# A gated-attention and MLP kernel: second unit's keys loaded alone, and the first 230 entries of a written order made anew

## Chip, cores and metric

The kernel runs on one core of a Trainium2 chip. The metric is the device time of one execution in microseconds (us). Engines are named as in the profile: PE (TensorE; PEld is its weight load), DVE (VectorE), ACT (ScalarE), POOL (GpSimd) and SP (SyncE, which here only issues DMAs).

## What is computed

A gated linear attention over 4 batches, 8 heads, 768 steps of 48 values feeds a gated two-layer MLP (3072 tokens, 384 to 2048 to 384). Cut to its core:

```python
f = 1 / (1 + exp(-f_logit))
for t in range(768):
    state = f[t] * state + outer(k[t], v[t])     # per batch and head, 48 x 48
    y[t] = q[t] @ state
x = y over all heads                              # 3072 tokens x 384
h = x @ w_in                                      # 384 -> 2048
g = h * clip(h + 3, 0, 6) / 6
out = g @ w_out                                   # 2048 -> 384
```

## The kernel before

**Units.** The attention is cut into 24 units, one batch and one chunk of 128 steps each. Units 0 to 3 are the first chunk of the four batches. For unit i, `load.i`, `loadq.i` and `loadv.i` are DMAs of gate logits, of queries with keys (one DMA of 512 KB into a tile `qkf`, rotated over four buffers) and of values. `loadq` of unit 0 is split: `loadk.0` brings its keys, `loadq.0` its queries.

On the engines a unit is this chain: ACT `gate` (sigmoid), DVE `back` (a scan of the gates backward, into `suffix`), `rend` (reciprocal of the end), `kmul` (keys times suffix, line 446), `fwd` (a forward scan, line 457), `qmul` (queries times it, line 463); PE `tk` (transposes keys, line 527), ACT `ktok` (copies them out), PE `kv` (keys by values, line 548), ACT `carry0`, `carry1`; PE `att` (keys by queries, line 508), DVE `mask` (line 515), PE `qs` (state part, line 583), `av` (line 599); then `xh`, `xs`, `xl` write the result as two float16 parts, and `hole` moves rows by DMA.

**Weights.** `ld.f` loads weight tile f (16 of them); ACT `cy`, `z`, DVE `mid`, `dif`, `top`, ACT `high` and DVE `lowi` turn it into two float16 parts. `high` gives the upper part, `lowi` the lower.

**MLP.** `mm1a.f` (line 844) multiplies units 0 and 1 by weight tile f, `mm1b.f` units 2 and 3; each is nine matmuls, of which only the last three read the lower weight part. `relua`, `ga` and `mm2a` (line 862) follow on ACT, DVE and PE. Later entries of the MLP have other names.

**Fillers.** `warm.n` (line 1087) is a matmul of zeros of n times 128 columns, n over 4 in pieces of 512; its result is not read. Each piece is two PE instructions in the profile, so `warm.16` is eight.

**Order.** One list of names, `ORDER`, fixes the order in which instructions are written. Every engine executes its own in that order, so an instruction that waits holds back all behind it on that engine; the engines meet by semaphores alone. A number after a second dot is the PSUM bank. `ON_POOL` names the entries that go to POOL instead of DVE; `kmul.1` is one of them.

Of the kernel before, what the change touches and what calls it, by code (L numbers as in the profile page):

```python
# [58 lines left out]
load.3 warm.3 kv.1.3 z.0 mid.0 loadq.2 gate.3 end.2 back.3 ld.1 carry0.1 warm.1 qs.1.0 dif.0 kmul.2 top.0 fwd.2 xl.0
carry1.1 loadq.3 av.1 hole.0 tk.2.4 rend.3 xh.1 xs.1 xl.1 z.1 qmul.2 warm.5 att.2.2 kmul.3 cy.1 mid.1 fwd.3 ktok.2  # L60
loadv.2 high.0 warm.4 kv.2.1 carry0.2 end.3 tk.3.4 ktok.3 mask.2 load.4 gate.4 qs.2.0 hole.1 av.2 xh.2 carry1.2 lowi.0
mm1a.0.4 relua.0 dif.1 qmul.3 top.1 high.1 ga.0 loadv.3 xs.2 att.3.2 mask.3 kv.3.1 ld.2 carry0.3 carry1.3 lowi.1 xl.2
loadq.4 warm.1 qs.3.2 av.3 xh.3 mm1a.1.4 cy.2 xs.3 xl.3 relua.1 z.2 back.4 kmul.4 rend.4 fwd.4 ga.1 decay.4 mm2a.0
qmul.4 load.5 gate.5 tk.4.1 mm2a.1 ktok.4 loadv.4 ld.3 cy.3 z.3 hole.2 mid.2 dif.2 top.2 att.4.2 kv.4.3 hole.3 mm1b.0.0
high.2 back.5 mid.3 relub.0 loadq.5 mm1b.1.1 relub.1 lowi.2 gb.0 dif.3 kmul.5 rend.5 gb.1 mm1a.2.4 mm1b.2.0 top.3
mm2b.0 mm2b.1 fwd.5 tk.5.1 relua.2 relub.2 gb.2 qmul.5 ld.4 z.4 cy.4 mid.4 mm2b.2 high.3 ktok.5 lowi.3 ga.2 mm1b.3.0
load.6 gate.6 loadq.6 dif.4 back.6 top.4 load.7 mm1a.3.4 ld.5 relub.3 mm2a.2 relua.3 ga.3 high.4 gb.3 cy.5 z.5 mask.4
mm2a.3 lowi.4 mm1a.4.1 relua.4 rend.6 ld.6 mm1b.4.4 relub.4 loadv.6 gate.7 loadq.7 mm2b.3 carry0.4 kmul.6 fwd.6 mid.5
ga.4 dif.5 z.6 qmul.6 top.5 cy.6 tk.6.1 ktok.6 mm2a.4 back.7 ld.7 decay.5 high.5 qs.4.2 decay.6 att.5.0 gb.4 av.4
kv.6.1 carry1.4 lowi.5 mm1.5.4 mask.5 mm2b.4 carry0.6 xh.4 z.7 xl.4 mid.6 dif.6 kmul.7 carry1.6 loadv.5 kv.5.3 ld.8  # L70
relu.5 g.5 mm2x.5 cy.7 top.6 high.6 cy.8 rend.7 tk.7.0 mid.7 dif.7 load.8 lowi.6 carry0.5 top.7 mm1.6.4 ktok.7 qs.5.2
fwd.7 qmul.7 high.7 loadv.7 relu.6 g.6 z.8 decay.7 att.6.0 ld.9 lowi.7 gate.8 av.5 cy.9 z.9 mask.6 mm1.7.4 relu.7 mid.8
dif.8 top.8 mid.9 carry1.5 dif.9 high.8 low.8 mm2x.6 mm1.8.0 g.7 loadq.8 ld.10 top.9 xh.5 cy.10 relu.8 high.9 back.8
rend.8 mm2x.7 ld.11 xl.5 g.8 att.7.2 z.10 cy.11 qs.6.0 kv.7.3 mid.10 load.10 loadv.8 av.6 dif.10 low.9 top.10 z.11
mid.11 gh.8 mm1.9.4 ld.12 ld.14 xh.6 xl.6 gl.8 mm2.8 dif.11 high.10 low.10 relu.9 g.9 cy.12 mm1.10.1 top.11 mask.7
kmul.8 carry0.7 gh.9 gl.9 hole.4 relu.10 high.11 mm2.9 carry1.7 g.10 low.11 z.12 mid.12 ld.13 dif.12 top.12 cy.13 gh.10
gl.10 tk.8.1 ktok.8 mm1.11.0 z.13 high.12 qs.7.2 mm2.10 av.7 loadq.9 ld.15 kv.8.3 decay.8 relu.11 mid.13 dif.13 low.12
loadv.9 mm1.12.1 g.11 gh.11 xh.7 top.13 carry0.8 high.13 xl.7 hole.7 gl.11 relu.12 z.14 z.15 low.13 fwd.8 qmul.8 mm2.11
g.12 gh.12 mm1.13.4 relu.13 g.13 cy.14 gh.13 gl.13 gl.12 mm2.12 cy.15 qs.8.2 mid.14 dif.14 att.8.0 mask.8 lowo.0 top.14
high.14 hole.6 hole.5 mm1.16.4 load.9 mid.15 mm1.17.1 relu.16 carry1.8 relu.17 dif.15 ws1.0 g.16 mm1.20.0 g.17 loadq.11  # L80
low.14 gate.10 xtop.0 gate.9 mm1.18.1 load.11 top.15 relu.18 loadq.10 back.9 high.15 gh.16 av.8 back.10 mm1.14.4 g.18
mm2.13 lowo.4 gh.17 relu.14 low.15 g.14 gh.14 mm1.15.1 mm1.19.4 lowo.6 gh.18 kmul.9 gl.18 rend.9 relu.15 g.15 lowo.3
gh.15 gl.14 gl.15 tk.9.1 lowo.5 lowo.1 mm2.14 fwd.9 mm2.15 gl.16 ktok.9 gl.17 outs.2 loadv.11 lowo.7 outv.1 outs.0
mm1.23.1 mm2.16 gate.11 lowo.2 ws2.0 relu.19 od.0 ws3.0 mm2.17 rend.10 xh.8 g.19 back.11 od.2 kmul.10 relu.20 decay.9
relu.23 kmul.11 hole.8 fwd.10 rend.11 od.1 load.13 qmul.10 xsum.0.2 g.20 g.23 mm1.21.4 relu.21 load.12 xleast.0 tk.10.3
ws4.0 qmul.9 decay.10 ktok.10 mm2.18 gh.19 g.21 mm1.25.3 gh.20 mm1.24.2 gh.21 loadv.10 gate.12 wtop.4 gl.19 relu.24
att.9.1 relu.25 kv.9.0 gl.20 fwd.11 g.25 carry0.9 loadv.12 g.24 wsh.0 load.14 qmul.11 mm1.22.4 gate.13 relu.22 back.12
gh.24 mm2.19 tk.11.3 gl.21 ws1.1 mask.9 gh.23 carry1.9 ktok.11 mm2.20 g.22 qs.9.0 att.11.3 gate.14 loadq.12 gh.25 gl.25
av.9 att.10.2 mm2.21 back.13 gh.22 xh.9 gl.23 kv.11.0 rend.12 kv.10.1 gl.22 mask.10 loadq.13 decay.11 mm1.26.4 ws2.1
mask.11 carry0.10 qs.10.3 ws3.1 carry0.11 carry1.10 kmul.12 kmul.13 fwd.12 qs.11.1 av.10 av.11 relu.26 mm2.22 ws4.1  # L90
xh.10 xh.11 decay.12 rend.13 mm1.27.3 gl.24 carry1.11 relu.27 loadq.14 decay.13 fwd.13 tk.12.2 mm1.28.1 relu.28 hole.9
ktok.12 wsl.0 ws1.2 g.27 tk.13.0 mm2.23 qmul.12 qmul.13 wsh.1 hole.10 att.13.3 ws2.2 g.26 ktok.13 g.28 xtop.1 att.12.1
t0.4 loadv.13 kv.12.2 kv.13.0 back.14 carry0.13 load.15 hole.11 load.16 xsum.1.4 carry0.12 gh.26 mm2.24 gh.27 mm2.25
t0.5 mask.13 carry1.12 t1.4 t1.5 seed.0.2 kmul.14 mm1.30.3 gh.28 t2.4 ws3.2 xleast.1 carry1.13 t2.5 th.4 ws4.2 gate.15
mask.12 gl.26 gl.27 wsl.1 th.5 ws1.3 mm2.26 tl.4 mm1.29.1 tk.14.2 relu.30 mm1.31.0 tl.5 relu.29 rend.14 g.30 p1.8.4
loadv.14 ktok.14 ws2.3 relu.31 p7.8.2 g.29 wsh.2 cs.8 ca.8.2 loadv.17 mm2.27 g.31 p6.8 gh.29 gate.16 fwd.14 qs.13.0
xtop.2 cx.8.3 qs.12.1 p2.8 wsl.2 ws3.3 ra.8 back.15 gl.28 p5.8 av.13 av.12 mm2.28 gh.31 gaw.8 loadq.15 loadq.17 gh.30
ws4.3 rend.15 load.17 ce.8 wsh.3 p4.8 qmul.14 gl.30 gl.29 xh.13 xh.12 p3.8 p8.8 rb.8 rx.8 p7.9.1 decay.14 wsl.3 mm2.29
gl.31 kmul.15 loadq.16 re.8 tk.15.0 gew.8 cs.9 p1.9.4 gbw.8 ca.9.2 mm2.30 fwd.15 loadv.15 gxw.8 back.16 ktok.15
xsum.2.1 mm2.31 p6.9 qmul.15 p7.11.0 xmost.2 gh.33 gh.34 cs.11 xleast.2 p2.9 decay.15 gl.34 hole.13 gh.32 kv.15.1  # L100
kv.14.0 kmul.16 cx.9.3 gl.32 outs.5 load.18 ra.9 hole.12 carry0.14 carry1.14 p4.9 carry0.15 outs.3 carry1.15 p5.9 rx.9
att.14.0 gaw.9 att.15.1 ce.9 outv.4 gate.17 p8.9 mask.14 rend.16 p3.9 mask.15 gh.35 gate.18 qs.15.0 back.17 re.9
qs.14.1 gxw.9 fwd.16 kmul.17 gl.33 gl.35 mm2.32 av.14 av.15 gew.9 p7.10.3 xh.15 rend.17 loadq.18 mm2.33 mm2.34 t0.6
p1.10.4 rb.9 mm2.35 gbw.9 qmul.16 fwd.17 xh.14 loadv.16 back.18 gh.37 gh.38 rend.18 cs.10 decay.16 load.19 kmul.18
ca.10.2 gl.38 hole.15 p6.10 gh.36 tk.17.0 gl.37 p2.10 hole.14 decay.17 tk.16.1 gh.39 cx.10.3 gl.36 p4.10 t1.6 gate.19
fwd.18 ra.10 gaw.10 t2.6 ktok.17 p5.10 ktok.16 att.16.0 kv.16.1 mm2.36 ce.10 t0.7 qmul.17 p8.10 load.20 rx.10 re.10
load.21 qmul.18 back.19 loadv.18 p3.10 mm2.37 rb.10 mask.16 gew.10 carry0.16 carry1.16 p1.11.4 gbw.10 gh.40 att.17.0
gxw.10 kv.17.1 t1.7 th.6 loadq.19 ca.11.2 gl.40 gl.39 mm2.38 gh.42 p6.11 t2.7 carry0.17 xtop.3 carry1.17 gl.42 gate.21
# [1146 lines left out]
```

## Time and profile before

| what | value |
|---|---|
| median of 3 runs | 457.13 us (456.36 to 457.28) |
| the profiled execution, device time | 456.43 us |
| its span, first to last instruction | 454.7 us |
| PE busy | 446.9 us, 98% of the span |
| DVE, ACT, POOL busy | 357.5, 232.1, 18.7 us |
| granted TensorE clock, mean | 1.000 |

The span leaves out 1.7 us of the device time around the first and last instruction. A busy PE is not PE at its peak, and fillers count as busy too. Starts and durations in the rows are in us from the span's start. A DVE or ACT row's duration runs some 0.1 us past the start of an independent follower, since such instructions overlap at their ends.

### The profile page before, as it was taken

Reading aid. Unit: us, or ns where it says so; the run is one execution under the profiler, and the core shown is the slowest. Engines: PE = TensorE matmul, PEld = TensorE weight load, DVE = VectorE, ACT = ScalarE, POOL = GpSimd, SP = SyncE. Lnnn points to the kernel's source line nnn. Section 1 sums busy time; section 2 is a strip of 40 time slices with the busy share of each in tenths; the row PEclk is TensorE's granted clock in tenths of the full one; section 3 lists DMA queues with packets and bytes.
Section 4 is the critical chain, followed back from the end, with each engine's and each line's share of the span. In section 5 each row is a group of like instructions: output and inputs, shape, how many; then the busy total and the mean of one; then the engine's idle time right before and its main releaser. Section 6 shows DMA issues by size and latency. Waiting matters only on the chain.

```text
span 454.7 us, 12561 instructions
## 1 busy us (share of the span) xinstructions
PE 446.9 (98%) x5449; PEld 290.4 (64%) x5449; DVE 357.5 (79%) x639; ACT 232.1 (51%) x393; POOL 18.7 (4%) x31
## 2 busy tenths in 40 slices
...
GB/s 281 252 237 404 201 208 240 200 172 0 62 135 80 180 31 100 69 9 115 91 0 85 99 139 1 25 140 1 2 10 1 7 28 1 1 115 2 1 0 74
DMA packets 25675, 43.18 MB, mean 95 GB/s; under 512 B 2576, under 2 KB 17424, under 8 KB 25616
## 3 DMA queue, kind: packets, MB, share of 16 engines
...
q8 instruction: 43, 0.70, 0.6%
...
q14 instruction: 16, 0.13, 0.1%
...
## 4 chain that ended last, share of the span: by engine, by line
PE 95%; DMA 1%; DVE 1%; SPq 1%; ACT 1%; issue 0%; POOL 0%; POOLq 0%
PE o L725 36%; PE pair L788 16%; PE single L788 9%; PE pair L676 7%; PE single L676 5%; PE o L862 3%; PE pair L508 3%; PE pair L599 3%; PE pair L583 3%; PE pair L548 2%; PE o L736 2%; PE pair L527 2%; DMA qkf<-qk 1%; PE o_half L878 1%; PE pair L878 1%; PE single L844 1%
## 5 line engine op out<-in xcount | busy, mean ns | idle before, releaser
L725 PE MATMUL o<-gg,weight 128*128 128x512 f16 x744 | 173.4, 379 | 0.0
L725 PEld LDWEIGHTS <-weight 128*128 128x128 f16 x744 | 71.7, 98 | 73.8
L788 PEld LDWEIGHTS <-weight 128*128 128x128 f16 x672 | 65.0, 98 | 13.2
L788 PE MATMUL pair<-xmem,wide 128*128 128x256 f16 x384 | 51.2, 273 | 0.0
L699 ACT ACTIVATE gg<-raws 128x512 f16<-128x512 f32 x64 | 38.6, 626 | 22.8 <-PE o_half L878 7.2
L788 PE MATMUL single<-xmem,weight 128*128 128x256 f16 x384 | 49.8, 273 | 0.0
L817 ACT ACTIVATE raws<-pair,half 128x512 f32<-128x512 f32 x32 | 21.6, 687 | 42.5 <-PE pair L788 33.6
L788 PEld LDWEIGHTS <-wide 128*128 128x128 f16 x384 | 36.9, 98 | 8.7 <-DVE single L803 0.6
L817 ACT ACTIVATE raws<-single,half 128x512 f32<-128x512 f32 x32 | 22.0, 689 | 38.4 <-PE single L788 37.4
L676 PEld LDWEIGHTS <-weight 128*128 128x128 f16 x243 | 23.1, 98 | 26.7 <-issue 0.3
L788 PE MATMUL pair<-xmem,weight 128*128 128x256 f16 x288 | 36.5, 273 | 0.0
L709 DVE TENSOR_TENSOR gg<-raws,gg 128x512 f16<-128x512 f32 x48 | 31.9, 684 | 5.2 <-ACT gg L699 5.1
L822 DVE SCALAR_TENSOR_TENSOR raws<-raws,single 128x512 f32<-128x512 f32 x32 | 21.8, 683 | 17.5 <-ACT raws L817 17.5
L676 PE MATMUL pair<-xmem,weight 128*128 128x512 f16 x144 | 33.2, 379 | 0.0
L803 DVE TENSOR_TENSOR pair<-pair,raws 128x512 f32<-128x512 f32 x16 | 11.1, 696 | 26.7 <-PE pair L788 23.6
L457 DVE TENSOR_TENSOR_SCAN suffix<-gates,rend 112x516 f32<-112x516 f32 x24 | 29.7, 1237 | 0.8 <-POOL qkf L446 0.7
L822 DVE SCALAR_TENSOR_TENSOR raws<-raws,pair 128x512 f32<-128x512 f32 x32 | 21.5, 681 | 10.6 <-ACT raws L817 10.4
L433 DVE TENSOR_TENSOR_SCAN suffix<-gates,unit 112x516 f32<-112x516 f32 x23 | 28.1, 1224 | 0.0
L676 PE MATMUL single<-xmem,weight 128*128 128x512 f16 x99 | 23.2, 380 | 0.0
L686 ACT ACTIVATE tg<-pair,half 128x512 f32<-128x512 f32 x16 | 10.9, 688 | 19.4 <-PE pair L676 16.2
L699 ACT ACTIVATE gg<-tg 128x512 f16<-128x512 f32 x24 | 14.4, 627 | 8.9 <-DVE tg L690 5.2
L515 DVE TENSOR_TENSOR a<-pair,causal 128x512 f32<-128x512 f32 x24 | 16.3, 683 | 1.9 <-PE pair L548 1.0
...
## 6 DMA issues: line engine op xcount, KB each, us to landing
...
gates<-fg SPq DMA_DIRECT2D x23, 258.5 KB, 3.4
...
```

Of the source, the lines that this page charges most:

```text
L433: nc.vector.tensor_tensor_scan(flat(sf)[:, ::-1], gt[:, 1:][:, ::-1], flat(unit)[:, ::-1], 0.0, op0=ALU.mult, op1=ALU.add,)
L457: nc.vector.tensor_tensor_scan(flat(sf), gt[:, :NP * (C + 1)], flat(rend), 0.0, op0=ALU.mult, op1=ALU.add,)
L508: nc.tensor.matmul(d["at"][HC * odd:HC * (odd + 1), e, 2 * n + c], t[rs, 1, n, c, odd], t[rs, 0, n, c, odd], start=not growing[at], stop=T ...
L515: nc.vector.tensor_tensor(d["a"].rearrange("r p e t -> r e p t"), d["at"], causal.unsqueeze(1).unsqueeze(1).broadcast_to([128, 2, NP, HC]) ...
L583: nc.tensor.matmul(d["y"][to:to + m, odd, n, cs], before[rs, p, :m], t[rs, 0, n, c, odd], start=alone and (odd, e) not in seen, stop=False ...
L676: nc.tensor.matmul(h, win[:, f, a, k * 128:(k + 1) * 128], g["xt"][:, k, :g["n"] // C, b], start=i == 0, stop=i == 3 * KT - 1,)
L699: nc.scalar.activation(as_t(d, 0), d["t"], AF.Copy)
L709: engine("gl", int(g["name"]) * NF + f).tensor_tensor(as_t(d, 1), d["t"], as_t(d, 0), op=ALU.subtract)
L725: nc.tensor.matmul(g["o"][m], wout[:, f, a, m * 128:(m + 1) * 128], g[f]["gg"][:, b], start=f == 0 and i == 0, stop=f == NF - 1 and i == 2 ...
L788: nc.tensor.matmul(to[:, n * 256:(n + 1) * 256], weights(q, n, a), g["wide"][:, :, block - 3, b], start=fresh and count == 1, stop=count = ...
L817: nc.scalar.activation(to, src, AF.Relu, bias=half, scale=RISE)
L822: nc.vector.scalar_tensor_tensor(to, to, TOP, src, op0=ALU.min, op1=ALU.mult)
```

## The change

The order list has one more entry, `loadk.1`, and its first 230 entries (229 before) stand in another order. From `cy.6 tk.6.1 ktok.6` on, its last 1335 entries are the same, one by one. The fillers are the same ten, but six more of them stand ahead of `tk.0`. `loadk` is offered for unit 1 too, so that unit 1's keys and queries come in two DMAs of 256 KB, the keys ahead of unit 2's gates. `kmul.1` leaves `ON_POOL` and is done on DVE.

```diff
 ON_POOL = """
-kmul.1 decay.4 kmul.6 lowi.5 kmul.7 decay.7 lowi.7 kmul.8 gl.9 decay.8 gl.11 qmul.8 gl.12 lowo.0 low.14
+decay.4 kmul.6 lowi.5 kmul.7 decay.7 lowi.7 kmul.8 gl.9 decay.8 gl.11 qmul.8 gl.12 lowo.0 low.14
 """.split()
 ORDER = """
-load.0 loadh.0 gate.0 gateh.0 back.0 backh.0 loadk.0 load.1 loadv.0 loadq.0 rend.0 end.0 kmul.0 fwd.0 gate.1 back.1
-warm.16 tk.0.3 ktok.0 warm.4 kv.0.1 carry0.0 load.2 qmul.0 warm.1 att.0.0 loadq.1 ld.0 rend.1 qs.0.2 mask.0 gate.2
...
+load.0 loadh.0 gate.0 gateh.0 back.0 backh.0 loadk.0 load.1 loadv.0 loadq.0 rend.0 gate.1 warm.16 warm.4 warm.1 warm.1
+kmul.0 warm.3 end.0 warm.3 warm.1 tk.0.3 loadk.1 load.2 loadq.1 ktok.0 fwd.0 loadq.2 loadv.1 load.3 back.1 warm.5
...
@@ -413,7 +413,7 @@
         def loadq():
-            if i:
+            if i > 1:
                 loadk(slice(0, 2))
             else:
                 nc.sync.dma_start(out=whole[i][:, 0], in_=qk[u][:, 0])
@@ -474,7 +474,9 @@
         if i == 0:
-            ops.update(halved(sf, gt, rows), loadk=loadk)
+            ops.update(halved(sf, gt, rows))
+        if i < 2:
+            ops["loadk"] = loadk
```

The DMAs on SP near the program's start, as a difference. `qkf_137` is unit 0's tile of queries and keys, `qkf_204` (before) and `qkf_161` (now) unit 1's, `qkf_168` unit 2's, `gates_80` unit 2's gates.

```order
 L423 DMA v_140<-v 128x400
 L419 DMA qkf_137<-qk 128x512
+L412 DMA qkf_161<-qk 128x512
 L408 DMA gates_80<-fg 128x517
-L412 DMA qkf_204<-qk 128x1024
+L419 DMA qkf_161<-qk 128x512
+L412 DMA qkf_168<-qk 128x1024
+L423 DMA v_170<-v 128x400
```

Unit 1's keys now go out one place earlier and alone, its queries follow unit 2's gates, and unit 2's tile comes ahead of the first weight tile, which moves behind the units' loads.

PE at its start, before: fillers (`idle`), the transposes `tk.0`, a filler, and the first two of `kv.0`.

```order
L1087 MATMUL idle<-blank 128x512 x4
L527 MATMUL pair_71<-ident,qkf_137 128x112 x4
L1087 MATMUL idle<-blank 128x512
L548 MATMUL pair_70<-v_140,ktok_157 64x48
L548 MATMUL pair_70<-v_140,ktok_157 48x48
```

PE at its start, now, to the same place:

```order
L1089 MATMUL idle<-blank 128x512 x5
L1089 MATMUL idle<-blank 128x128 x2
L1089 MATMUL idle<-blank 128x384 x2
L1089 MATMUL idle<-blank 128x128
L529 MATMUL pair_71<-ident,qkf_137 128x112 x4
L1089 MATMUL idle<-blank 128x512
L1089 MATMUL idle<-blank 128x128
L550 MATMUL pair_70<-v_140,ktok_165 64x48
```

Six fillers (one of 512 columns, three of 128, two of 384) moved ahead of `tk.0`, and the one between `tk.0` and `kv.0` is longer by 128 columns. Behind `kv.0` no filler is left until `av.2`, where before there were seven.

DVE from unit 1's `back` to unit 1's reciprocal and mask, before (`a_216` and `a_271` are what `mask.0` and `mask.1` write):

```order
L433 SCALAR_TENSOR_TENSOR suffix_79<-gates_78,unit 112x516
L463 TENSOR_TENSOR qkf_137<-qkf_137,suffix_77 112x512
L451 RECIPROCAL rend<-suffix_79 112x4
L515 TENSOR_TENSOR a_216<-pair_70,causal 128x2x4x64
L457 SCALAR_TENSOR_TENSOR suffix_79<-gates_78,rend 112x516
L463 TENSOR_TENSOR qkf_204<-qkf_204,suffix_79 112x512
L433 SCALAR_TENSOR_TENSOR suffix_81<-gates_80,unit 112x516
L515 TENSOR_TENSOR a_271<-pair_70,causal 128x2x4x64
```

The same stretch of DVE now, where the two masks write `a_237` and `a_279`:

```order
L433 SCALAR_TENSOR_TENSOR suffix_79<-gates_78,unit 112x516
L463 TENSOR_TENSOR qkf_137<-qkf_137,suffix_77 112x512
L451 RECIPROCAL rend<-suffix_79 112x4
L446 TENSOR_TENSOR qkf_161<-qkf_161,suffix_79 112x512
L457 SCALAR_TENSOR_TENSOR suffix_79<-gates_78,rend 112x516
L517 TENSOR_TENSOR a_237<-pair_70,causal 128x2x4x64
L463 TENSOR_TENSOR qkf_161<-qkf_161,suffix_79 112x512
L433 SCALAR_TENSOR_TENSOR suffix_81<-gates_80,unit 112x516
L517 TENSOR_TENSOR a_279<-pair_70,causal 128x2x4x64
```

`kmul.1` (line 446) is new on DVE, and `fwd.1` stands ahead of `mask.0`. Further on, all DVE work of units 2 and 3 down to `mask.2` stands ahead of `mid.0`, the first weight entry on DVE. The next DVE entries are `mid.0 qmul.3 dif.0 top.0 mid.1 dif.1 top.1 lowi.0 mask.3 back.4 ga.0 lowi.1`, where before `mid.0` followed `rend.2`, and `back.4` stood behind `lowi.1`.

## Rows read from the trace of the kernel before

**Rows 1.** Windows: busy time of each engine, granted clock, DMA share, GB/s.

```profile
28.86:50.37 21.51, 21.51 (x211) 18.54 (x205) 20.89 (x42) 16.59 (x28) 2.30 (x2) 1.00 0.72 277
```

**Rows 2.** Chain that ended last, 3 to 14 us: start, us, what.

```profile
3.62 0.43 SPq L408
...
4.09 5.57 DMA qkf<-qk
...
9.80 1.19 POOL qkf L446
```

**Rows 3.** DMA issues between 3.6 and 4 us: size, us to landing.

```profile
gates<-fg SPq DMA_DIRECT2D x1, 258.5 KB, 4.8
```

**Rows 4.** Timeline of PE: start, us, instructions, idle before and its releaser.

```profile
1.13 5.09 PE L1087 MATMUL idle<-blank 128*128 128x512 f32 x8 [1.13 <-DVE blank L246]
...
6.05 0.55 PE L527 MATMUL pair<-ident,qkf 112*128 112x112 f32 x4
...
6.44 1.04 PE L1087 MATMUL idle<-blank 128*128 128x512 f32 x2
...
7.40 0.91 PE L548 MATMUL pair<-v,ktok 64*64 64x48 f32 x48
...
8.24 0.49 PE L1087 MATMUL idle<-blank 128*128 128x128 f32 x2
...
8.77 0.69 PE L508 MATMUL pair<-qkf 48*64 48x64 f32 x32
...
13.13 0.69 PE L508 MATMUL pair<-qkf 48*64 48x64 f32 x32 [0.82 <-DVE qkf L463]
...
27.70 0.46 PE L583 MATMUL pair<-qkf,middle 48*64 48x64 f32 x16
...
28.25 0.69 PE L599 MATMUL pair<-a,v 64*64 64x64 f32 x32
...
28.86 1.16 PE L844 MATMUL single<-xmem,weight 128*128 128x256 f16 x9
```

**Rows 5.** Timeline of PEld: two weight loads of the first filler.

```profile
4.33 0.19 PEld L1087 LDWEIGHTS idle<-blank 128*128 128x128 f32 x1 [0.24 <-issue]
4.76 0.19 PEld L1087 LDWEIGHTS idle<-blank 128*128 128x128 f32 x1 [0.24 <-issue]
```

**Rows 6.** Timeline of DVE.

```profile
5.00 0.67 DVE L446 TENSOR_TENSOR qkf<-qkf,suffix 112x512 f32<-112x512 f32 x1
5.70 1.23 DVE L457 TENSOR_TENSOR_SCAN suffix<-gates,rend 112x516 f32<-112x516 f32 x1
6.85 1.21 DVE L433 TENSOR_TENSOR_SCAN suffix<-gates,unit 112x516 f32<-112x516 f32 x1
7.97 0.67 DVE L463 TENSOR_TENSOR qkf<-qkf,suffix 112x512 f32<-112x512 f32 x1
8.55 0.18 DVE L451 RECIPROCAL rend<-suffix 112x4 f32<-112x4 f32 x1
9.60 0.69 DVE L515 TENSOR_TENSOR a<-pair,causal 128x512 f32<-128x512 f32 x1 [0.87 <-PE pair L508]
...
26.21 0.42 DVE L857 SCALAR_TENSOR_TENSOR th<-th,single 128x256 f32<-128x256 f32 x1 [0.88 <-ACT th L853]
...
27.24 0.55 DVE L319 TENSOR_TENSOR weight<-wide,weight 128x384 f16<-128x384 f32 x1
...
32.31 0.35 DVE L300 TENSOR_SCALAR raws<-top 128x768 int16<-128x768 int16 x1
32.69 0.56 DVE L307 TENSOR_TENSOR top<-top,raws 128x768 int16<-128x768 int16 x1
33.28 1.07 DVE L311 SCALAR_TENSOR_TENSOR wide<-top,wide 128x768 int16<-128x768 int16 x1
```

**Rows 7.** Timeline of ACT: `ktok.0` and `gate.2`.

```profile
6.64 0.55 ACT L534 ACTIVATE ktok<-pair 128x448 f32<-128x448 f32 x1 [0.40 <-PE pair L527]
...
8.61 0.62 ACT L427 ACTIVATE gates<-gates 112x512 f32<-112x512 f32 x1
```

More of the change, by code (lines that the diff above doesn't have):

```diff
@@ L59 @@
[L59 to L108, printed above, removed]
@@ L144 @@
-gl.89 p2.23 mm2p.87 mm2m1.89 cx.23.3 ra.23 p5.23 mm2p.88 gaw.23 mm2m0.87 gl.90 ce.23 p4.23 mm2q.87 p3.23 xmost.5
+load.0 loadh.0 gate.0 gateh.0 back.0 backh.0 loadk.0 load.1 loadv.0 loadq.0 rend.0 gate.1 warm.16 warm.4 warm.1 warm.1
+kmul.0 warm.3 end.0 warm.3 warm.1 tk.0.3 loadk.1 load.2 loadq.1 ktok.0 fwd.0 loadq.2 loadv.1 load.3 back.1 warm.5
+qmul.0 rend.1 kv.0.1 att.0.0 carry1.0 carry0.0 kmul.1 tk.1.4 qs.0.2 fwd.1 end.1 loadq.3 mask.0 ktok.1 av.0 qmul.1
+att.1.0 gate.2 back.2 ld.0 xh.0 mask.1 xs.0 kv.1.3 carry0.1 rend.2 end.2 loadv.2 qs.1.0 av.1 kmul.2 tk.2.4 gate.3 fwd.2
@@ new lines @@
+xl.0 carry1.1 ld.1 xh.1 ktok.2 xs.1 xl.1 back.3 z.0 qmul.2 hole.0 load.4 rend.3 kmul.3 fwd.3 cy.0 att.2.2 kv.2.1
+loadv.3 carry1.2 loadv.4 tk.3.4 mask.2 carry0.2 mid.0 qmul.3 qs.2.0 dif.0 att.3.2 hole.1 loadq.4 av.2 cy.1 z.1 top.0
+ld.2 ld.3 xh.2 warm.4 warm.1 xs.2 mid.1 dif.1 top.1 ktok.3 kv.3.1 high.0 gate.4 carry0.3 lowi.0 mm1a.0.4 mask.3 qs.3.2
+high.1 relua.0 back.4 ga.0 lowi.1 av.3 mm1a.1.4 end.3 rend.4 carry1.3 kmul.4 fwd.4 xl.2 load.5 hole.2 xh.3 z.2 relua.1
+ga.1 xs.3 xl.3 hole.3 cy.2 ld.4 qmul.4 mm2a.0 mid.2 dif.2 tk.4.1 z.3 mm2a.1 top.2 ktok.4 gate.5 back.5 cy.3 high.2
@@ new lines @@
+mid.3 att.4.2 lowi.2 kv.4.3 mm1b.0.0 relub.0 gb.0 mm1b.1.1 dif.3 top.3 relub.1 gb.1 mm1a.2.4 relua.2 loadq.5 high.3
+mm1b.2.0 relub.2 ga.2 mm2b.0 rend.5 kmul.5 z.4 ld.5 mm2a.2 load.6 ld.6 tk.5.1 loadq.6 loadq.7 cy.4 cy.5 loadv.6 fwd.5
+z.5 lowi.3 mid.4 gb.2 dif.4 gate.6 ktok.5 top.4 high.4 mm2b.1 mm1b.3.0 back.6 decay.4 relub.3 lowi.4 mid.5 kmul.6 gb.3
+mm2b.2 mm1a.3.4 rend.6 load.7 mask.4 dif.5 mm1a.4.1 relua.3 ga.3 relua.4 mm2b.3 mm1b.4.4 mm2a.3 ga.4 relub.4 top.5
+fwd.6 qmul.5 carry0.4 qmul.6 gate.7 z.6 cy.6 tk.6.1 ktok.6 mm2a.4 back.7 ld.7 decay.5 high.5 qs.4.2 decay.6 att.5.0
@@ new lines @@
+gb.4 av.4 kv.6.1 carry1.4 lowi.5 mm1.5.4 mask.5 mm2b.4 carry0.6 xh.4 z.7 xl.4 mid.6 dif.6 kmul.7 carry1.6 loadv.5
+kv.5.3 ld.8 relu.5 g.5 mm2x.5 cy.7 top.6 high.6 cy.8 rend.7 tk.7.0 mid.7 dif.7 load.8 lowi.6 carry0.5 top.7 mm1.6.4
+ktok.7 qs.5.2 fwd.7 qmul.7 high.7 loadv.7 relu.6 g.6 z.8 decay.7 att.6.0 ld.9 lowi.7 gate.8 av.5 cy.9 z.9 mask.6
+mm1.7.4 relu.7 mid.8 dif.8 top.8 mid.9 carry1.5 dif.9 high.8 low.8 mm2x.6 mm1.8.0 g.7 loadq.8 ld.10 top.9 xh.5 cy.10
+relu.8 high.9 back.8 rend.8 mm2x.7 ld.11 xl.5 g.8 att.7.2 z.10 cy.11 qs.6.0 kv.7.3 mid.10 load.10 loadv.8 av.6 dif.10
@@ new lines @@
+low.9 top.10 z.11 mid.11 gh.8 mm1.9.4 ld.12 ld.14 xh.6 xl.6 gl.8 mm2.8 dif.11 high.10 low.10 relu.9 g.9 cy.12 mm1.10.1
+top.11 mask.7 kmul.8 carry0.7 gh.9 gl.9 hole.4 relu.10 high.11 mm2.9 carry1.7 g.10 low.11 z.12 mid.12 ld.13 dif.12
+top.12 cy.13 gh.10 gl.10 tk.8.1 ktok.8 mm1.11.0 z.13 high.12 qs.7.2 mm2.10 av.7 loadq.9 ld.15 kv.8.3 decay.8 relu.11
+mid.13 dif.13 low.12 loadv.9 mm1.12.1 g.11 gh.11 xh.7 top.13 carry0.8 high.13 xl.7 hole.7 gl.11 relu.12 z.14 z.15
+low.13 fwd.8 qmul.8 mm2.11 g.12 gh.12 mm1.13.4 relu.13 g.13 cy.14 gh.13 gl.13 gl.12 mm2.12 cy.15 qs.8.2 mid.14 dif.14
```

101 lines of the change are left out of this document (65 added, 36 removed).

## The prediction, on record before the result

> **What bounds the kernel now.** I read the windows first. From 28.86 us on, PE is busy without a gap: 21.51 of the 21.51 us to 50.37 [rows 1], and so on to the last weight products; at 50.37 us stands `tk.6`, with which the unchanged part of the order begins. So the end comes a fixed stretch of PE work after PE last waits, and a change to the first 230 entries moves the end by what it moves that moment, here `mm1a.1` at 28.86 [rows 4]. DVE is nearly as full there (20.89 of 21.51), so a late DVE can make PE wait again; both have to be followed.
>
> Next I read the chain. Ahead of 13.13 us it runs back over unit 1: its 512 KB of keys and queries are issued at 4.09 and land 5.57 later, at 9.66; POOL multiplies the keys from 9.80 for 1.19 [rows 2]; then DVE runs `fwd.1` and `qmul.1`, and PE, idle for 0.82, starts `att.1` at 13.13 [rows 4]. Fillers lie in these holes, so PE's real slack ahead of 28.86 is larger than its idle time. The timelines give the durations.
>
> **The change: the key load and `kmul.1`.** `loadk.1` (256 KB) takes the queue place of unit 2's gates (258.5 KB), which are issued at 3.62 and land 4.8 later [rows 2, 3]: 8.4 us. Unit 1's reciprocal starts at 8.55 [rows 6], so `kmul.1` runs on DVE from 8.64 for about 0.67 instead of ending on POOL at 10.99, and `fwd.1` behind it is done 8.55 + 0.09 + 0.70 + 1.15 = 10.49, each step being the distance of two starts [rows 6]. The tile is ready 1.7 us earlier. The extra DMA is one more issue on SP; nobody waits for what it pushes back, since unit 2 is needed at about 15 us and the first weight tile only behind `mask.2`. [...]
>
> **The fillers ahead of `tk.0`.** Now PE is what holds unit 0 back. Two instructions of 512 columns start 0.43 apart [rows 5], and one of fewer columns in proportion: `warm.4` is 0.86, three `warm.1` 0.64, two `warm.3` 1.29, together 2.80 (rounded sum). At most a hand-over of 0.10 is added to each of the six (6.44 to 7.40 is 0.96 for 0.86 [rows 4]), so 3.4; I take 2.80, since loads run ahead of matmuls. `tk.0` moves from 6.05 to 8.85; `kmul.0` is done at 5.67 [rows 6], so nothing else holds it. Then `tk.0` 0.39, `warm.5` 1.07, a hand-over 0.10, `kv.0` 0.84 [rows 4, 5]: `att.0` starts at 8.85 + 2.40 = 11.25 (8.77 before). `mask.0` starts 0.83 after `att.0` (9.60 after 8.77 [rows 4, 6]): 12.08. So DVE is idle from 10.49 to 12.08, and most of what the early keys gave is spent.
>
> **ACT's order makes `back.2` late.** `gate.2` now stands behind `ktok.1`. `att.0` takes PE 0.62 (its 0.69 less the 0.07 by which such a row runs past the next start, as 0.91 to 0.84), so `tk.1` is at 11.87; `ktok` starts 0.59 after `tk` (6.64 after 6.05), takes 0.45 to the next start, and the gate takes 0.62 [rows 4, 7]: 13.53, `back.2` at 13.55. DVE would be there at 12.08 + 0.60 + 0.58 = 13.26. This costs 0.29; if ACT is quicker it costs nothing.
>
> **DVE from `back.2` to `ga.0`.** From here DVE has no wait that I can find. By start distances [rows 6], and a duration less 0.09 where the follower is independent (0.67 to 0.58 at 7.97): three `back` at 1.12, three `mask` 0.60, two `rend` 0.09, two `kmul` 0.70, two `fwd` 1.15, two `qmul` 0.58, `mid.0` 0.26, `mid.1` 0.38, two `dif` 0.59, two `top` 0.98, `lowi.0` 0.46: 14.44 us for 21 instructions. `ga.0` starts at 27.99, is done at 28.41 (0.42), and `mm1a.1`, which reuses its bank, starts at 28.45. It need not wait for `lowi.1` (done at 28.9): only its last three matmuls read the lower part, 0.65 after its start. If it did wait from the start, it would start at 28.92; this is the upper bound of this term.
>
> **PE's own way there.** `qmul.3` starts 8.16 into that chain, at 21.71, so `att.3` at about 22.4. From there `att` 0.62, `av` 0.61 (28.86 less 28.25), the last two fillers 1.07, `xs` about 0.3, `kv` 0.84, `mm1a.0` about 0.97 (nine times a quarter of 0.43), `qs` 0.55 (28.25 less 27.70), `av` 0.61 [rows 4, 5]: 28.0, with a hand-over at each small piece up to 28.4. So PE and DVE meet there almost together.
>
> **Behind `mm1a.1`** the same PE entries stand as before up to `tk.6` in a slightly other order: 21.51 us of work. DVE has `back.4` behind it already, so its next `lowi` come no later against PE than before.
>
> **Sum.** 28.45 less 28.86 is -0.41 us. The profiled execution took 456.43; that gives 456.0. It lay 0.70 below the median of the runs, 457.13, so I expect a median of 456.7. A measurement of this kernel can tell about 0.2%, 0.91 us, from no change: the forecast is no change. Bounds of its own terms: -0.29 if `gate.2` is not late; +0.6 for the fillers and +0.47 if `mm1a.1` waits for `lowi.1`. That is 456.4 to 457.8.
>
> **Rival, faster: the clock rises earlier.** The first filler's eight instructions take 4.92 us from 1.13 to 6.05 [rows 4]; at 0.43 each they would take 3.44. [...] Before, this time had cover: `att.1` waited for `qmul.1` until 13.13 whatever the fillers did. Now every instruction done at full pace moves `tk.0`, `att.0` and `mask.0` by 0.43, until DVE's 10.49 is reached. Two more at full pace give -0.41 - 0.86 = -1.27: 455.9. It decides from 0.5 us of earlier rise. [...] 0.2.
>
> **Rival, slower: the same exposure, or ACT.** Three more instructions at half pace give -0.41 + 1.29 = +0.88, with any of the filler hand-overs over the 0.91: 458.1. This is one mechanism with its place, the start of `tk.0`, and decides from 1.3 us of delay there. [...] A different one would be DVE as the new bound: it now carries `kmul.1` as well, and if each of its 21 hand-overs took 0.06 more, `ga.0` would be 1.3 late, 458.0; the row distances, taken in the same code, speak against it. I give 0.2 to this side, mostly to the first.
>
> **Rival, within no change: it does not do what it says.** The keys come earlier and nothing uses it, because `att.0` is later by 2.5 us; the fillers are the same work in another place. That is the forecast's own mechanism, with the result anywhere from -0.7 to +0.7 us. 0.6 for all of it.
>
> **Numbers.** Faster by over 0.2% 0.2, within 0.6, slower 0.2. The range takes in the own bounds and reaches halfway into both rivals: 455.7 to 458.3.
>
> **What would show it.** In the changed kernel's profile: `tk.0` near 8.85 with fillers back to back ahead of it; `kmul.1` on DVE at 8.6; DVE idle for about 1.6 us ahead of `mask.0` at 12.1, put down to PE; a short idle ahead of `back.2`, put down to ACT; hardly any DVE idle from 13.6 to 28; `mm1a.1` at about 28.45; `tk.6` at about 50.0. It would be wrong if `tk.0` came outside 8.4 to 9.6, if DVE waited for the weight entries of ACT (`cy`, `z`, `high`), which now stand behind the units' copies, if a weight tile landed too late, its DMA being issued behind the units' loads, or if PE had new gaps behind 28.5, for instance at `mm1a.2`, which needs `lowi.2`.

## The result, and the profile after

The changed kernel takes 459.86 us (median of 10 executions, 458.32 to 463.46), the kernel before beside it 456.42 (456.12 to 457.36, also 10): a ratio of 1.0076, 95% interval 1.006 to 1.0092. The forecast was 456.7 us, no change, with a range up to 458.3. It was wrong: the change costs 3.4 us.

The profiled execution of the changed kernel took 459.83 us, its span is 458.0 (454.7 before). The same timeline of PE as in [rows 4], from the first filler to `mm1a.1`, and the entry `tk.6` with which the unchanged part of the order begins:

```profile
1.13 9.27 PE L1089 MATMUL idle<-blank 128*128 128x512 f32 x20 [1.13 <-DVE blank L246]
10.24 0.55 PE L529 MATMUL pair<-ident,qkf 112*128 112x112 f32 x4
...
12.45 0.27 PE L510 MATMUL pair<-qkf 48*64 48x64 f32 x2
...
12.55 0.65 PE L510 MATMUL pair<-qkf 48*64 48x64 f32 x30
...
16.36 0.66 PE L550 MATMUL pair<-v,ktok 64*64 64x48 f32 x26
18.52 0.55 PE L550 MATMUL pair<-v,ktok 64*48 64x48 f32 x22 [1.49 <-issue]
19.55 0.46 PE L585 MATMUL pair<-qkf,middle 48*64 48x64 f32 x16 [0.48 <-issue]
20.09 0.94 PE L601 MATMUL pair<-a,v 64*64 64x64 f32 x32
...
31.64 1.14 PE L846 MATMUL single<-xmem,weight 128*128 128x256 f16 x9
...
53.80 0.55 PE L529 MATMUL pair<-ident,qkf 112*128 112x112 f32 x4
```

`tk.0` starts at 10.24 (6.05 in [rows 4]), `mm1a.1` at 31.64 (28.86), `tk.6` at 53.80 (50.37); the span is 3.3 longer, so all of the loss lies ahead of `tk.6`. The new thing stands in the middle. `kv.1` is 48 matmuls of one kind with all its inputs there. PE does 26 of them, then nothing for 1.49 us (its stand, below), then the other 22, and the idle time is put down to "issue": it waits for nothing that the profile shows. Behind it the same `av` that takes 0.69 takes 0.94. (The 0.48 ahead of `qs.1` is another matter: ACT's `carry0.1` has to run between `kv.1` and `qs.1`, and no filler stands there any more.)

Windows of the same stretch (busy us and count of PE, PEld, DVE, ACT, POOL; then granted clock, DMA share, GB/s):

```profile
14.00:16.00 2.00, 1.73 (x80) 1.39 (x80) 2.00 (x3) 1.47 (x3) 0.00 (x0) 1.00 1.07 437
16.00:18.00 2.00, 1.02 (x28) 0.71 (x28) 1.97 (x5) 0.00 (x0) 0.00 (x0) 1.00 0.17 57
18.00:20.00 2.00, 1.00 (x38) 0.78 (x38) 0.81 (x1) 0.88 (x4) 0.00 (x0) 1.00 0.00 0
20.00:22.00 2.00, 1.92 (x41) 1.64 (x38) 1.90 (x4) 1.37 (x4) 0.00 (x0) 0.59 0.03 10
22.00:24.00 2.00, 2.00 (x74) 1.66 (x75) 1.97 (x4) 2.00 (x4) 0.00 (x0) 0.55 0.30 79
```

The DMA engines' share is 1.07 in 14 to 16 us and 0.17 in 16 to 18, PE is idle for half of 16 to 20, and then the granted clock falls: 0.59 and 0.55 of full speed in the next two windows, the trace's clock record being 0.50 from 20.37 to 23.79 us. In the kernel before it reads 1.00 in each of these five windows. DVE and ACT meet the stand too. Timeline of DVE (`mask.0`, `back.2`, `back.3`, `ga.0`):

```profile
13.86 0.69 DVE L517 TENSOR_TENSOR a<-pair,causal 128x512 f32<-128x512 f32 x1 [3.30 <-ACT middle L563]
...
15.07 1.23 DVE L433 TENSOR_TENSOR_SCAN suffix<-gates,unit 112x516 f32<-112x516 f32 x1
...
20.10 1.23 DVE L433 TENSOR_TENSOR_SCAN suffix<-gates,unit 112x516 f32<-112x516 f32 x1 [1.29 <-ACT gates L427]
...
31.16 0.42 DVE L859 SCALAR_TENSOR_TENSOR th<-th,single 128x256 f32<-128x256 f32 x1
```

`back.3` waits 1.29 for `gate.3`, which stands on ACT behind `carry0.1`, which waits for the halted `kv.1`:

```profile
19.12 0.33 ACT L563 ACTIVATE middle<-pair 112x192 f32<-112x192 f32 x1 [3.17 <-PE pair L550]
```

**A packet near the stand.** The DMA view lists a queue of packets of 16384 bytes, kind "instruction", 43 in the whole run (0.70 MB). In the changed kernel the first of them comes in the window 16 to 18 us; in the kernel before it came in the window 12 to 14. The two views, after and then before:

```profile
q1 hardware_dynamic: 32, 0.10, 13.6%
q8 instruction: 1, 0.02, 3.4%
```

```profile
q1 hardware_dynamic: 184, 0.82, 100.5%
q8 instruction: 1, 0.02, 3.1%
```

Taken one by one from the trace, the packet runs from 16.16 to 17.25 after and from 12.31 to 13.31 before. The trace has a record for nearly every instruction of PE. The last one ahead of its stand is the 449th (220 matmuls, 220 weight loads and 9 semaphore and drain instructions; the expectations call the place the 229th matmul), and PE goes on 1.27 us after the packet is in. In the kernel before, PE comes to its 449th record at 15.17, 1.86 us after its packet was in, and does not stop.

**Theories.** These are guesses; what the packet brings stands in no view. *Instruction stream:* it brings the instructions behind the 449th record (the expectations call what stands ahead of them PE's first block of code); PE, now fed without holes, gets there before the packet has come through DMA engines full of data (share 1.07 in 14 to 16 us), and stands; then the clock falls. *Fillers:* the six fillers ahead of `tk.0` hold unit 0 back and leave none for later. *ACT's order:* `gate.3` behind `carry0.1` stops DVE. *The split itself.*

### The profile page after: what moved, and what is told of

The parts are those of the page before. It is cut to its first block, busy times and chain, and to the rows that moved or that the text cites. A ratio compares the mean times of both kernels' runs of the same rounds, so it can differ in the third digit from the quotient of the medians.

```text
span 458.0 us, 12557 instructions
## 1 busy us (share of the span) xinstructions
PE 448.9 (98%) x5445; PEld 292.4 (64%) x5449; DVE 358.8 (78%) x640; ACT 231.2 (50%) x393; POOL 17.9 (4%) x30
## 4 chain that ended last, share of the span: by engine, by line
PE 91%; DVE 4%; DMA 1%; issue 1%; ACT 1%; SPq 0%; DVEq 0%
PE o L727 35%; PE pair L790 16%; PE single L790 9%; PE pair L678 7%; PE single L678 5%; PE pair L601 3%; PE pair L585 2%; PE pair L510 2%; PE idle L1089 2%; PE pair L550 2%; PE o L738 2%; DMA qkf<-qk 1%; PE pair L529 1%; PE o_half L880 1%; PE pair L880 1%
```

## Experiments

"Before" in the ratios is the kernel before, run on the same chip in the same rounds. Edits of the order show a few neighbours only.

### The split alone, and fillers moved

The order of before with the split and `kmul.1` on DVE:

```diff
 ORDER of before
-... loadk.0 load.1 loadv.0 loadq.0 rend.0 ...
+... loadk.0 load.1 loadv.0 loadq.0 loadk.1 rend.0 ...
-... ld.0 rend.1 qs.0.2 ... xh.0 kmul.1 tk.1.4 ...
+... ld.0 rend.1 kmul.1 qs.0.2 ... xh.0 tk.1.4 ...
```

> The written order of the kernel before, with only the split: the second unit's keys have a load of their own (issued behind the first unit's queries) and their k product runs on VectorE behind rend.1; filler matmuls stay where the kernel before has them. If the split and the VectorE product are harmless and the new order is what costs (theories of the fillers and of the instruction stream), 455.9 to 456.4 us, no slower than before (456.4), att.1 starting about 12.2 us. If the split itself is what costs, 458 us or more, near the changed kernel's 459.9.

Measured 456.67 us against 456.69, ratio 0.9999 (0.999 to 1.0009). The split is harmless, and useless (456.67 lies above the expected 455.9 to 456.4, but so does the kernel before beside it): `att.1` starts at 12.94 instead of 13.13, 0.7 later than I expected, and PE even stops at the same record for a moment:

```profile
14.57 0.72 PE L550 MATMUL pair<-v,ktok 64*64 64x48 f32 x33
15.80 0.44 PE L550 MATMUL pair<-v,ktok 64*64 64x48 f32 x15 [0.51 <-issue]
```

This 0.51 us does not show in the time. So the new order costs, not the split.

The changed kernel with its fillers behind the PE entries of before:

```diff
-gate.1 warm.16 warm.4 warm.1 warm.1 kmul.0 warm.3 end.0 warm.3 warm.1 tk.0.3 ... warm.5 qmul.0 rend.1 kv.0.1
+gate.1 warm.16 kmul.0 end.0 tk.0.3 warm.4 ... qmul.0 rend.1 kv.0.1 warm.1
...
```

> The changed kernel with its filler matmuls put back behind the same PE entries as in the kernel before. Filler theory (fillers ahead of tk.0 delay unit 0 and use up the cover that PE had later): tk.0 starts at 6 to 7 us, about 456.4 us in all. Instruction stream theory (PE without holes runs ahead of its code, whose fetch waits behind the data): the fillers make little difference, PE still stands more than 1 us inside kv.1, 459 to 460 us.

459.8 us, ratio 1.0061 (1.0039 to 1.0083), seven executions from 457.33 to 461.35. `tk.0` starts at 6.49, 3.75 us earlier than in the changed kernel, and nothing is gained: PE stands longer at its 449th record:

```profile
14.13 0.67 PE L550 MATMUL pair<-v,ktok 64*64 64x48 f32 x32
17.25 0.44 PE L550 MATMUL pair<-v,ktok 64*64 64x48 f32 x16 [2.44 <-issue]
```

The changed kernel without the six early fillers (12 matmul records in the profile, not the 13 of the expectation):

```diff
-gate.1 warm.16 warm.4 warm.1 warm.1 kmul.0 warm.3 end.0 warm.3 warm.1 tk.0.3
+gate.1 warm.16 kmul.0 end.0 tk.0.3
```

> The changed kernel without the six filler entries ahead of tk.0 (13 filler matmuls are left out; nothing reads their result). Filler theory: tk.0 starts at 6 to 7 us and the time falls to 457 us or less. Instruction stream theory: PE comes to the end of its first block of code later or earlier by those matmuls but the fetch still waits for the data, a stand of about 1 us remains, 459 us or more.

457.95 us, ratio 1.0025 (1.0009 to 1.004): between the numbers of the two theories, with twelve executions from 455.79 to 459.75. In the profiled one, which took 459.33, PE gets to the place at 13.85 and stands until 17.59:

```profile
13.27 0.79 PE L550 MATMUL pair<-v,ktok 64*64 64x48 f32 x38
17.59 0.56 PE L550 MATMUL pair<-v,ktok 64*48 64x48 f32 x10 [3.53 <-issue]
```

and the granted clock reads 0.50 for 10 us:

```profile
15.60:25.90 10.30, 7.76 (x179) 6.47 (x182) 6.20 (x11) 6.49 (x14) 0.00 (x0) 0.50 0.40 122
```

In these three PE is at its 449th record at 16.81, 14.59 and 13.85 and goes on at 18.52, 17.25 and 17.59. How early it is there moves little when it goes on. Still, the time is 1.9 us better than the changed kernel's, and the intervals do not meet, so the six fillers cost something of their own.

### The loads out of the way

The first two weight tiles issued by SP behind unit 0's last rows:

```diff
-... back.2 ld.0 xh.0 ... xl.0 carry1.1 ld.1 xh.1 ... qmul.2 hole.0 load.4 ...
+... back.2 xh.0 ... xl.0 hole.0 ld.0 ld.1 carry1.1 xh.1 ... qmul.2 load.4 ...
```

> The changed kernel with the two loads of the first weight tiles (ld.0, ld.1) issued on SP behind unit 0's last load, so that the DMA queues are not full of weights when PE comes to the end of its first block of code. Instruction stream theory: the 1.5 us stand inside kv.1 is gone or under 0.3 us, the clock does not fall behind it, about 457 us. Filler theory: tk.0 still starts near 10 us and the time stays at 459 to 460 us.

463.03 us, ratio 1.0136 (1.0118 to 1.0154). The stand in `kv.1` is gone, as the instruction stream theory has it (its packet came at 13.29), but my edit made a wait of its own: `hole.0` let the loads out only at 19.70, and ACT stood for the first tile, with PE idle for 4.58 us behind it:

```profile
24.38 0.89 ACT L287 ACTIVATE wide<-raws 128x768 int32<-128x768 uint32 x1 [4.13 <-DMA raws<-w]
```

So the time says nothing on the theory. The next edit puts the same loads where, by my estimate from these timelines, they are late enough for the packet and early enough for ACT:

```diff
-nc.sync.dma_start(out=raw[:, 1:4 * WN + 1], in_=w[f].bitcast(I16))
+(nc.scalar if f < 2 else nc.sync).dma_start(out=raw[:, 1:4 * WN + 1], in_=w[f].bitcast(I16))
 ORDER
-... att.1.0 gate.2 back.2 ld.0 xh.0 ... carry1.1 ld.1 xh.1 ...
+... att.1.0 gate.2 ld.0 ld.1 back.2 xh.0 ... carry1.1 xh.1 ...
```

> [...] Instruction stream theory: the stand of 1.49 us behind the 229th matmul falls below 0.6 us, the clock does not fall, 456 to 457.3 us. Filler theory: tk.0 still starts near 10 us and the time stays at 459 to 460.

458.07 us, ratio 1.0039 (1.0021 to 1.0058); 1.8 us of the 3.4 are back, and 0.8 are missing to the upper end of what I expected. In the profile `kv.1` runs through, and the granted clock reads 1.00:

```profile
16.25 0.91 PE L550 MATMUL pair<-v,ktok 64*64 64x48 f32 x48
17.66 0.46 PE L585 MATMUL pair<-qkf,middle 48*64 48x64 f32 x16 [0.50 <-issue]
...
29.77 1.14 PE L846 MATMUL single<-xmem,weight 128*128 128x256 f16 x9
...
52.50 0.55 PE L529 MATMUL pair<-ident,qkf 112*128 112x112 f32 x4
```

```profile
16.00:24.00 8.00, 5.88 (x212) 4.52 (x216) 7.93 (x14) 6.63 (x14) 0.00 (x0) 1.00 0.68 246
```

DVE is busy for 7.93 of 8 us here. Of the twelve executions the seven up to 458.18 us have a mean granted clock of 1.000, the five from 458.38 one of 0.992 to 0.995. The seven have a median of 457.16. The profile is of the first kind, so what the five did is not shown.

The same loads by ACT, without the six early fillers:

```diff
-gate.1 warm.16 warm.4 warm.1 warm.1 kmul.0 warm.3 end.0 warm.3 warm.1 tk.0.3
+gate.1 warm.16 kmul.0 end.0 tk.0.3
-... att.1.0 gate.2 back.2 ld.0 xh.0 ...
+... att.1.0 gate.2 ld.0 ld.1 back.2 xh.0 ...
```

> The same two loads issued by ACT, and the six filler entries ahead of tk.0 left out (nothing reads them). Instruction stream theory: the stand of 3.53 us that the kernel without those fillers has behind its 229th matmul falls below 1.5 us, 455 to 456.5 us, at or below the kernel before. If the stand is not the fetch behind the data, it stays above 3 us and the time near 458.

457.01 us, ratio 1.0016 (0.9994 to 1.0038), executions from 455.13 to 459.93. The stand falls from 3.53 to 0.81 us, as expected, but the median does not get below the kernel before; the two can't be told apart.

The same loads by ACT, with the fillers where before has them:

```diff
-gate.1 warm.16 warm.4 warm.1 warm.1 kmul.0 warm.3 end.0 warm.3 warm.1 tk.0.3 ... warm.5 qmul.0 rend.1 kv.0.1
+gate.1 warm.16 kmul.0 end.0 tk.0.3 warm.4 ... qmul.0 rend.1 kv.0.1 warm.1
-... att.1.0 gate.2 back.2 ld.0 xh.0 ...
+... att.1.0 gate.2 ld.0 ld.1 back.2 xh.0 ...
```

> The changed kernel with both answers: the filler matmuls back behind the PE entries of the kernel before, and ld.0, ld.1 issued by ACT behind gate.2. [...] Both theories together: no stand over 0.6 us, clock at full pace, tk.0 near 6.5, 455 to 456.5 us. If the fillers' place has no part in it, the time is that of the loads by ACT alone, 458.

460.73 us, ratio 1.0051 (1.0024 to 1.0079), and neither theory's number: the twelve executions of this one kernel fall into two groups, five from 456.27 to 457.63 us and seven from 460.54 to 461.84. The profiled one took 461.84. Its timeline and windows:

```profile
15.27 0.68 PE L550 MATMUL pair<-v,ktok 64*64 64x48 f32 x32
19.18 0.67 PE L550 MATMUL pair<-v,ktok 64*64 64x48 f32 x16 [3.24 <-issue]
```

```profile
16.00:19.00 3.00, 0.00 (x0) 0.00 (x0) 0.71 (x1) 0.00 (x0) 0.00 (x0) 0.73 0.57 229
19.00:24.00 5.00, 4.73 (x73) 3.91 (x74) 3.06 (x5) 2.84 (x8) 0.00 (x0) 0.50 0.05 13
```

ACT issued the weights at 11.51 and 11.95, and the instruction packet ran from 16.79 to 17.75. The next kernel differs only in `ld.2`, and its profile is of the other kind:

```diff
-... tk.2.4 gate.3 fwd.2 ... z.1 top.0 ld.2 ld.3 xh.2 ...
+... tk.2.4 gate.3 ld.2 fwd.2 ... z.1 top.0 ld.3 xh.2 ...
```

> The same with the third weight tile (ld.2) issued by ACT behind gate.3 instead of by SP behind a store that waits for unit 0's and 1's rows. In the run with the loads by ACT alone ACT stood 0.80 us for that tile at 31.09 and PE 0.74 us behind it for ktok.4. If that is what is lost between mm1a.1 and tk.6, the time falls by 0.4 to 0.8 us against the kernel without it, to 454.5 to 456; if not, it stays the same.

457.51 us, ratio 1.0033 (1.0009 to 1.0056); nine executions from 456.01 to 457.97, three from 460.67 to 461.58. The packet ran from 13.21 to 14.19, and PE waits 0.21:

```profile
14.76 0.68 PE L550 MATMUL pair<-v,ktok 64*64 64x48 f32 x32
15.65 0.44 PE L550 MATMUL pair<-v,ktok 64*64 64x48 f32 x16 [0.21 <-issue]
```

So up to that point one order of instructions has its packet at 13.21 in one profile and at 16.79 us in the other, which would fit a race with the weights' packets (not shown), and the profile with the late packet shows a stand of 3.24 us and a clock of 0.50 behind it. The medians of the two groups of the kernel before this one are 456.63 and 461.01; that all of a group's executions are like its one profile is inferred. The earlier `ld.2` did not bring its 0.4 to 0.8 us (its nine faster executions have a median of 457.34): ACT no longer stands for the tile, but DVE now waits for ACT at `back.3` (0.94) and `mid.1` (0.96), and ACT for `kv.2` (1.48).

Two last ones, from the kernel without early fillers, put `ld.0` and `ld.1` behind `xh.0`, `ld.2` behind `gate.3`, all by ACT, and in the second `ld.3` behind `xh.2`:

```diff
-... gate.2 ld.0 ld.1 back.2 xh.0 mask.1 ... tk.2.4 gate.3 fwd.2 ... top.0 ld.2 ld.3 xh.2 ...
+... gate.2 back.2 xh.0 ld.0 ld.1 mask.1 ... tk.2.4 gate.3 ld.2 fwd.2 ... top.0 ld.3 xh.2 ...
 in the second
+... top.0 xh.2 ld.3 ...
```

> The kernel with ld.0, ld.1 by ACT and without the six early filler entries (457.01, its executions from 455.1 to 459.9), with ld.0 and ld.1 now behind xh.0 on ACT (about 13 us) instead of behind ktok.1 (11.3 and 11.7, where the two earlier kernels came in two groups of executions some 4 us apart), and ld.2 by ACT behind gate.3. Instruction stream theory: the code is asked for at about 11.6 us, well ahead of the weights, in every execution: one group, no stand over 0.6 us, the median near the fast end of the kernel it is made from, 455 to 456 us. If the two groups come from something else (the clock at the start), they stay and the median stays at 457.

> The same with ld.3 by ACT behind xh.2 as well, so that ACT no longer stands for that tile (0.71 us at 32.98 in the run it goes back to). If what is lost behind mm1a.1 is ACT waiting for weights, 0.3 to 0.7 us less than without it; if not, the same.

458.92 us (1.0052, 1.0038 to 1.0065) and 459.52 (1.0063, 1.0049 to 1.0077). Expected were 455 to 456 and less. Each has one group of executions, at the slow end of the kernel they are made from. In the first the weights went out at 12.61, the packet came only at 14.37, PE stood 2.34 us and the clock fell (mean 0.993 over the profile). In the second, the same up to there, the packet came at 13.25, PE stood 1.39 us and the clock fell too (mean 0.988). The 11.6 us at which the code is asked for was an estimate that no run shows; what the two profiles show is packets at 14.37 and 13.25, and a stand in both. The second kernel also stopped again in `kv.2`, for 1.19 us, behind the 705th record, which is 256 behind the 449th; its second packet was in at 21.06, 1.58 us before PE went on:

```profile
20.41 1.04 PE L550 MATMUL pair<-v,ktok 64*64 64x48 f32 x30
22.64 0.68 PE L550 MATMUL pair<-v,ktok 64*48 64x48 f32 x18 [1.19 <-issue]
```

### ACT's order, and more data in the queue

```diff
-... xs.0 kv.1.3 carry0.1 ... tk.2.4 gate.3 fwd.2 ...
+... xs.0 kv.1.3 gate.3 carry0.1 ... tk.2.4 fwd.2 ...
```

> The changed kernel with gate.3 ahead of carry0.1 on ACT, so that back.3 need not wait for ACT behind PE's stand (1.29 us of DVE idle). Theory of ACT's order: back.3 starts about 18.8 instead of 20.10 and the time falls by 0.8 to 1.3 us, to about 458.7. Instruction stream theory: PE's stand and the fallen clock hold units 1 to 3 back anyway; below 0.5 us of change, 459.4 to 460.

459.83 us, ratio 1.0065 (1.005 to 1.0081): nothing gained. `back.3` starts 2.16 us earlier, at 17.94, and DVE then waits 2.16 us for PE:

```profile
17.94 1.21 DVE L433 TENSOR_TENSOR_SCAN suffix<-gates,unit 112x516 f32<-112x516 f32 x1
...
23.82 0.69 DVE L517 TENSOR_TENSOR a<-pair,causal 128x512 f32<-128x512 f32 x1 [2.16 <-PE pair L510]
```

ACT's order is a place through which the loss runs, not its cause.

The kernel of the split alone with a third weight tile in the queue:

```diff
-... carry1.1 loadq.3 av.1 hole.0 ... kv.3.1 ld.2 carry0.3 ...
+... carry1.1 loadq.3 ld.2 av.1 hole.0 ... kv.3.1 carry0.3 ...
```

> The written order of the kernel before with the split (456.67 us), and the third weight tile (ld.2, 786 KB) issued early, behind loadq.3, which puts about 1.8 us more data into the queues that PE's code has to pass. Instruction stream theory: the code comes about 0.9 us later and the stand in kv.1 grows from 0.51 us to 1.2 us or more, with the clock falling behind it in some executions: 457 to 458.5 us. If the stand does not come from the data, a weight that lands early costs nothing: 456.4 to 456.8.

456.08 us, ratio 0.9992 (0.9983 to 1.0), and the expectation of the instruction stream theory is missed: `ld.2` was issued at 9.19, but the instruction packet ran from 13.30 to 14.26, no later than without it (13.48 to 14.50). So here the packet did not wait for all that SP had queued, and the third tile cost nothing here.

### The stops together

Counted from the records of the traces, in us. Eleven kernels stop, or pause, behind the 449th record:

| kernel | 449th record starts | instruction packet | PE goes on | packet's end to that |
|---|---|---|---|---|
| split alone | 15.07 | 13.48 to 14.50 | 15.80 | 1.30 |
| split, `ld.2` early | 15.39 | 13.30 to 14.26 | 15.73 | 1.47 |
| changed | 16.81 | 16.16 to 17.25 | 18.52 | 1.27 |
| fillers back | 14.59 | 14.99 to 15.97 | 17.25 | 1.28 |
| no early fillers | 13.85 | 15.04 to 16.10 | 17.59 | 1.49 |
| `gate.3` early | 16.03 | 15.86 to 16.86 | 18.29 | 1.43 |
| by ACT, no early fillers | 14.43 | 13.01 to 14.06 | 15.46 | 1.40 |
| by ACT, fillers back | 15.73 | 16.79 to 17.75 | 19.18 | 1.43 |
| the same, `ld.2` by ACT | 15.22 | 13.21 to 14.19 | 15.65 | 1.46 |
| loads behind `xh.0` | 14.18 | 14.37 to 15.36 | 16.74 | 1.38 |
| the same, `ld.3` by ACT | 14.07 | 13.25 to 14.21 | 15.67 | 1.46 |

In the three that do not stop the packet is in at 13.31 (before), 14.30 (weights late) and 14.58 (weights by ACT), and PE gets to the place 1.86, 1.87 and 2.00 us later. The eleven that stop were there at most 1.13 us after the packet's end, and whatever the order they go on 1.27 to 1.49 after it.

The 193rd record, 256 ahead of the 449th, starts 0.87 us ahead of the packet with the weights by ACT and 1.07 with the weights late, the two kernels that issue no weight tile before the packet comes. In the other twelve it starts 2.6 to 6.1 us ahead of the packet. This would fit a fetch that begins near that record and is held up by the weights; no view shows when one begins.

## Why the prediction was wrong, by its own steps

The median forecast stood 0.70 too high from the start: that was added for a median of three, and over ten executions the kernel before has 456.42, about the time of its profile. The steps are compared in the profiles. The prediction put `tk.6` at about 50.0, by its own steps at 28.45 + 21.51 = 49.96. It came at 53.80. The 3.84 us are, by where they arise:

| step | predicted | measured | adds |
|---|---|---|---|
| `tk.0` | 8.85 | 10.24 | 1.39 |
| `back.2` | 13.55 | 15.07 | 0.13 |
| `ga.0` | 27.99 | 31.16 | 1.65 |
| `mm1a.1` | 28.45 | 31.64 | 0.02 |
| `tk.6` | 49.96 | 53.80 | 0.65 |

**The fillers ahead of `tk.0`** were mis-sized: 2.80 us was to be added to the start of before, 4.19 was. The loads of the first filler instructions show why (PEld, 0.85 apart up to 6.41, 0.43 from 7.00 on):

```profile
5.56 0.33 PEld L1089 LDWEIGHTS idle<-blank 128*128 128x128 f32 x1 [0.52 <-issue]
6.41 0.33 PEld L1089 LDWEIGHTS idle<-blank 128*128 128x128 f32 x1 [0.52 <-issue]
7.00 0.19 PEld L1089 LDWEIGHTS idle<-blank 128*128 128x128 f32 x1 [0.25 <-issue]
7.43 0.19 PEld L1089 LDWEIGHTS idle<-blank 128*128 128x128 f32 x1 [0.24 <-issue]
```

In the kernel before the loads go over to 0.43 earlier, 0.85 apart up to 3.85 and 0.43 from 4.33 on [rows 5]:

```profile
3.00 0.34 PEld L1087 LDWEIGHTS idle<-blank 128*128 128x128 f32 x1 [0.52 <-issue]
3.85 0.25 PEld L1087 LDWEIGHTS idle<-blank 128*128 128x128 f32 x1 [0.52 <-issue]
```

The trace's first record of the granted clock, at 1.00, begins at 6.72 here and at 3.96 before; the windows read 1.00 ahead of it too, so the pace there is seen in the loads alone. At half pace the 2.76 us between the two do the work of 1.38, which is the 1.39. Over the fourteen profiles of this study that record begins between 3.96 and 7.33 us, PE having been idle up to 1.13 in all of them, and before's is the earliest of all, so the base of this term was one draw of many. The 0.43 us that both rivals put on one instruction at half pace is the difference of these distances, 0.85 less 0.43. The slower rival priced three more such instructions at 1.29; it gave 458.1, and is a part of the result, not the result.

**Unit 1's keys** were right: `kmul.1` at 8.63 (8.64), `fwd.1` at 9.33 with its follower free to start at 10.48 (10.49). The way from `tk.0` to `att.0` took 2.21 us (2.40). `mask.0` came 1.41 instead of 0.83 after `att.0`; the profile puts its wait down to `carry0.0` on ACT, which I had left out. On the other hand `gate.2` was not late.

**"From here DVE has no wait that I can find"** is the step that failed. The row sum was good: with the stand taken away by the loads on ACT, `back.2` to `ga.0` took 29.31 - 14.96 = 14.35 us (14.44 predicted):

```profile
14.96 1.22 DVE L433 TENSOR_TENSOR_SCAN suffix<-gates,unit 112x516 f32<-112x516 f32 x1
...
29.31 0.41 DVE L859 SCALAR_TENSOR_TENSOR th<-th,single 128x256 f32<-128x256 f32 x1
```

In the changed kernel it took 16.09, with 1.29 of it in the wait of `back.3` for ACT, which waited for PE in its stand, and 0.25 in a wait of `mid.0` for ACT. I asked of each PE entry which data it waits for, and the code itself did not occur to me. No rival held it.

**"Behind `mm1a.1`" the same 21.51 us** became 22.16. PE was busy for 21.80 of it. In the kernel with the loads by ACT it is 22.73, with ACT standing 0.80 us for `ld.2`'s tile. The rule of thumb that the end moves by what `mm1a.1` moves was good to 0.65 us only, more than the forecast gain.

**What the runs settle, and what not.** That PE's stop goes with the packet is shown: at one record in eleven kernels, PE going on 1.27 to 1.49 us behind the packet, with nothing else waited for that the profile shows, and no stop where the packet was in 1.86 us or more before PE got there. That the packet brings the code that PE lacks is my reading of its kind, "instruction", and of these times. That the order matters through this is shown by the loads on ACT (1.8 us back). It is not all: leaving out the six early fillers gave 1.9 us though PE stood longer in its profile, and with both edits the kernel can't be told from the kernel before. That the packet is late because of the data is shown only in part. With the weights by ACT it came at 13.50, the DMA engines' share being 0.09 in 13 to 14, and with weights in the queues at 14 to 17 in six kernels. But a third tile did not delay it, in the kernel before it came in good time through full engines (share 1.04 in 12 to 14), and with the loads behind `xh.0` it came late though their share was 0.78 in 12 to 13 and 0.70 in 13 to 14, the packet starting at 14.37. When the code is asked for, and which of the 16 engines brings it, stands in no view. How much of the loss is the stand and how much the lower clock behind it was not separated. For the rest of the loss once the stand is gone (458.07 against 456.49 us) its profile offers the late `tk.0` and ACT's wait for the third tile; neither is shown, and the third tile issued earlier gained nothing in the kernel with the fillers back.

No version beat the kernel before by more than can be measured; the nearest is the split with `ld.2` early, 0.9992 (0.9983 to 1.0).
